# A new order for scores, raw scores, products and exponentials in three kinds of phases of a fused attention and MLP kernel

## The chip, the cores and the metric

The kernel runs on one core of one Trainium2 chip. The metric is the device time of one execution in microseconds (us), as the median of several runs. Engines are named as the profile names them: PE is TensorE (matmuls), PEld its weight loads, ACT is ScalarE, DVE is VectorE, POOL is GpSimd, SP is SyncE (here it only issues DMAs).

## The reference

One sequence of 2048 rows of width 512 goes through multi-query attention (32 heads of 16, one shared key and value head) and through an MLP with a squared ReLU; a sigmoid gate per row mixes the two.

```python
q = (x @ wq).reshape(B, S, H, Dh).transpose(0, 2, 1, 3)
k, v = x @ wk, x @ wv
scores = einsum("bhqd,bkd->bhqk", q, k) * (Dh ** -0.5)
o = einsum("bhqk,bkd->bhqd", softmax(scores, -1), v)
a = o.transpose(0, 2, 1, 3).reshape(B, S, H * Dh) @ wo
r = where(x @ w1 + b1 > 0, x @ w1 + b1, 0)
b = (r * r) @ w2 + b2
g = sigmoid((x * gate_w).sum(-1, keepdims=True))
return g * a + (1 - g) * b          # S 2048, D 512, H 32, Dh 16, F 1792
```

## The kernel before

**Units.** The attention is cut into 1024 units. A unit is one tile of 128 keys against 256 queries of four heads. Its work has three steps: two score matmuls on PE (`score`, L880; one on rows 0 to 63 of the array and one on rows 64 to 127, called row 0 and row 1 here), one exponential over all 1024 columns on ACT (L917), and four context matmuls on PE that multiply the exponentials with the values and add into `acc` (L937). The context of a unit follows its scores by four units or more (`AHEAD`).

**Two ways for a score to leave PSUM.** Most units write both score halves into one tile `s` of two banks, of which there are two (`score_part`), and the exponential reads that tile. The pool hands the two tiles out in turn, so a unit's score must wait until the exponential of the unit two before it in that turn has read its tile. The other units are called raw scores: each half goes into `x`, a single bank (`score_copy`), DVE copies it to SBUF (L901), and the exponential later works in place in SBUF (`e<-e` in the profile). A half must wait until the copy of the half before it has read `x`.

**Products.** Beside the attention PE computes the projections and the MLP. A unit of that work is a list of 12 or 15 (sometimes 9) pairs of matmuls of half height (L1244): row 0 of the array works on the first half of the sum for one output and row 1 on the second half of the sum for the output before it. So PE's work comes in pairs: one matmul on row 0 and one on row 1 at the same time.

**Phases.** The program is a row of phases (`phase`). A phase of n units and m products first issues all its pairs, then the contexts of n units. The order of the pairs and that of the exponentials on ACT come from the table `PLANS`, written out by hand. Its key is (units, products, kind). Its text has one word per step: `M` is a product on both rows, `S3` a score of unit 3 of this phase on both rows, `06` the half on row 0 of unit 6 as a raw score, and `16` the half on row 1. Words that start with 0 go to row 0 alone, those with 1 to row 1 alone, all others to both; so a word with 1 shifts row 1 by one place against row 0 until a word with 0 evens it out. The tuple behind the text is the order in which ACT takes the units' exponentials. PE, ACT and DVE each run their instructions in the order in which the program writes them.

In this kernel 33 phases are (9, 15), 7 are (8, 15), 17 are (8, 12) and 67 are (7, 12); 12 others lie at the two ends. The planner's clocks (`at_pe`, `at_act`, `at_dve`) decide beside which raw score a small DVE operation is written (`spend`), from estimated costs.

After a phase's pairs, DVE does the closing work of the finished product (for a hidden MLP unit L763, L764, L203 and L204; for an output L786 or L228) and ACT may round a weight tile (L534). When the last context of a block of 256 queries is done, ACT copies half of `acc` (L991).

Of the kernel before, what the change touches and what calls it, by code (L numbers as in the profile page):

```python
# [39 lines left out]
WHOLE, FIRST, SECOND, LATER = range(4)  # L40
TAIL = {40: 8, 32: 8, 24: 5, 19: 5, 14: 5, 9: 5, 4: 4}
PLANS = {
    (9, 15, WHOLE): ("S0 16 M M S1 M M M 06 S2 M M S4 M M 13 M S5 M M M M S7 03 M S8", (0, 1, 2, 4, 5, 3, 8, 7, 6)),
    (8, 15, WHOLE): ("14 S0 M M S1 M M 04 M S2 M M M 13 S5 M M M M M 03 M S6 S7 M", (0, 1, 2, 5, 4, 3, 6, 7)),
    (7, 15, WHOLE): ("14 S0 M M S1 M M 04 M M S2 M M 13 M M M S5 M M M S6 M M 03", (0, 1, 2, 4, 5, 3, 6)),
    (8, 12, WHOLE): ("15 S0 M M S1 M M 05 M S2 M M M S4 13 M M S6 M M 03 S7", (0, 1, 2, 4, 5, 3, 6, 7)),
    (7, 12, WHOLE): ("14 S0 M M S1 M M 04 M M S2 M M 13 M M M S5 M S6 03", (0, 1, 2, 4, 5, 3, 6)),
    (6, 12, WHOLE): ("M 02 S0 M S1 M M M M M S3 M M M S4 12 M M S5", (0, 1, 3, 4, 5, 2)),
    (6, 12, LATER): ("S0 M M S1 M M M 02 M S3 M M M S4 M 12 M M S5", (0, 1, 3, 4, 5, 2)),
# [1409 lines left out]
```

## Time and profile before

| | |
|---|---|
| median of 3 runs | 1185.44 us (1181.39 to 1188.18) |
| profiled execution | 1181.19 us, of which the span from first to last instruction 1179.4 us |
| granted PE clock in it | 0.999 |
| PE busy | 1170.9 us (99% of the span) |
| ACT busy | 1025.9 us (87%) |
| DVE busy | 687.6 us (58%) |
| POOL busy | 71.2 us (6%) |

The profile is one execution. In a timeline row stand the start in us from the span's start, the length, the engine, the line, the operation, the tiles (out<-in), the shape and how many equal ones were merged, and in brackets the idle time of the engine before it with what ended it. In the table of groups stand busy time in us and the mean of one in ns. A matmul that waits for its buffer while it is at the head of PE's queue shows as a longer matmul.

### The profile page before, as it was taken

What the parts mean: (1) busy time and instruction counts of PE and PEld (TensorE: products, weight loads), DVE (VectorE), ACT (ScalarE), POOL (GpSimd) and SP (SyncE); (2) the same over time, 40 slices, a digit from 0 to 9 for tenths busy, and PEclk for the clock granted to TensorE, in tenths of its full rate; (3) what the DMA queues carried; (4) which work ended last, traced back from release to release, by engine and by line L of the source; (5) the groups of instructions that cost most, each with busy time, mean ns of one, the idle gap of its engine ahead of it and who ended that gap; (6) DMA issues with size and microseconds to landing.
All of it is one profiled execution on the core that took longest, in us unless ns stands there. A gap on an engine that the chain in (4) does not pass through costs nothing.

```text
span 1179.4 us, 31993 instructions
## 1 busy us (share of the span) xinstructions
PE 1170.9 (99%) x13807; PEld 775.6 (66%) x13807; DVE 687.6 (58%) x1154; ACT 1025.9 (87%) x1133; POOL 71.2 (6%) x128
## 2 busy tenths in 40 slices
PE   9999999999999999999999999999999999999997
PEld 4666666666666666666666666666666666666664
DVE  6887786764754745553666636535646437444553
ACT  7798899998988888889888898988888989889884
POOL 1010110010100000100000000001000000001000
PEclk9999999999999999999999999999999999999999
DMA  7455445251433514320524305224115224322101
GB/s 253 130 157 174 136 128 201 91 196 58 166 125 110 177 39 140 99 84 7 159 95 149 101 19 176 83 65 163 61 41 180 65 65 136 104 77 75 56 37 39
DMA packets 53802, 130.28 MB, mean 110 GB/s; under 512 B 14219, under 2 KB 14715, under 8 KB 53145
## 3 DMA queue, kind: packets, MB, share of 16 engines
q1 hardware_dynamic: 38712, 90.67, 24.4%
q0 software_dynamic: 14656, 37.19, 9.4%
q8 instruction: 110, 1.80, 0.6%
q14 instruction: 36, 0.29, 0.1%
q10 hardware_dynamic: 288, 0.33, 0.1%
HBM read 87.91 MB, written 35.64 MB: 105 GB/s over the span
## 4 chain that ended last, share of the span: by engine, by line
PE 98%; ACT 1%; DVE 0%; issue 0%; DVEq 0%; ACTq 0%
PE acc L937 39%; PE mm L1244 33%; PE s L880 19%; PE x L880 5%; ACT e L917 0%; PE acc L570 0%; PE mm L211 0%; PE mm L312 0%; DVE ot L1204 0%; DVE e L901 0%; PE s L321 0%; PE acc L357 0%; PE s L211 0%; PE acc L354 0%; PE s L312 0%
## 5 line engine op out<-in xcount | busy, mean ns | idle before, releaser
L917 ACT ACTIVATE e<-s 128x1024 f32<-128x1024 f32 x765 | 744.5, 1023 | 88.9 <-PE s L880 87.6
L901 DVE COPY e<-x 128x512 f32<-128x512 f32 x518 | 358.4, 692 | 448.6 <-PE x L880 323.3
L937 PE MATMUL acc<-e,v_ext 128*32 128x256 f32 x8192 | 470.2, 381 | 0.0
L880 PE MATMUL s<-qa,k_aug 49*128 49x512 f32 x1530 | 425.2, 413 | 0.1
L937 PEld LDWEIGHTS acc<-e,v_ext 128*32 128x32 f32 x8192 | 252.3, 110 | 190.5 <-issue 38.0
L917 ACT ACTIVATE e<-e 128x1024 f32<-128x1024 f32 x259 | 273.3, 1058 | 29.0 <-DVE e L901 29.0
L880 PEld LDWEIGHTS s<-qa,k_aug 49*128 49x128 f32 x1530 | 218.2, 184 | 103.5 <-ACT e L917 70.7
L1244 PE MATMUL mm<-w2p,hr 64*128 64x512 f32 x1128 | 243.4, 392 | 0.0
L880 PE MATMUL x<-qa,k_aug 49*128 49x512 f32 x518 | 213.4, 412 | 0.1
L1244 PEld LDWEIGHTS mm<-w2p,hr 64*128 64x128 f32 x1128 | 157.4, 186 | 18.0
L1244 PE MATMUL mm<-xragain,w1p 64*128 64x512 f32 x448 | 121.1, 394 | 0.0
L880 PEld LDWEIGHTS x<-qa,k_aug 49*128 49x128 f32 x518 | 95.2, 184 | 31.5 <-DVE e L901 13.6
L1244 PE MATMUL mm<-xr,w1p 64*128 64x512 f32 x448 | 115.7, 393 | 0.0
L1244 PEld LDWEIGHTS mm<-xragain,w1p 64*128 64x128 f32 x448 | 69.9, 186 | 5.8
L1244 PEld LDWEIGHTS mm<-xr,w1p 64*128 64x128 f32 x448 | 68.1, 186 | 6.3
L1244 PE MATMUL mm<-xlagain,w1p 64*128 64x512 f32 x224 | 68.0, 393 | 0.0
L1244 PE MATMUL mm<-xl,w1p 64*128 64x512 f32 x224 | 65.3, 392 | 0.0
L1244 PE MATMUL mm<-more 64*128 64x512 f32 x216 | 59.4, 393 | 0.0
L763 DVE TENSOR_SCALAR big<-mm,b1t 128x512 f32<-128x512 f32 x56 | 41.6, 743 | 0.5 <-PE mm L1244 0.5
L764 DVE TENSOR_TENSOR big<-big 128x512 f32<-128x512 f32 x56 | 38.8, 692 | 1.9
L1244 PE MATMUL mm<-wor,orr 64*128 64x512 f32 x120 | 38.4, 393 | 0.0
L1244 PE MATMUL mm<-wor,orl 64*128 64x512 f32 x120 | 38.1, 391 | 0.0
(187 smaller groups left out, 797.8 us busy)
## 6 DMA issues: line engine op xcount, KB each, us to landing
w1p<-w1kept SPq DMA_DIRECT2D x42, 512.0 KB
w2p<-w2kept SPq DMA_DIRECT2D x35, 512.0 KB
qa<-qs SPq DMA_DIRECT2D x186, 64.0 KB
w1kept<-w1p POOLq DMA_DIRECT2D x14, 512.0 KB, 4.3
w2kept<-w2p POOLq DMA_DIRECT2D x12, 512.0 KB, 5.9
qs<-qr SPq DMA_DIRECT2D x16, 256.0 KB
ress<-res POOLq DMA_DIRECT2D x4, 1024.0 KB, 4.7
qs<-ql POOLq DMA_DIRECT2D x15, 256.0 KB, 8.1
```

The source lines that it names most:

```text
L763: nc.vector.tensor_scalar(h[0], p, b1t[:, f:f + 1], 0.0, op0=OP.add, op1=OP.max)
L764: nc.vector.tensor_tensor(h[0], h[0], h[0], OP.mult)
L880: nc.tensor.matmul(dst.rearrange("p (a n) -> p a n", a=2), k_aug[rows, kt * 128:(kt + 1) * 128], qa[it][rows, :, q * HC:q * HC + HC], star ...
L901: nc.vector.tensor_copy(e_half(u)[:, 2 * r:2 * r + 2], x.rearrange("p (a n) -> p a n", a=2))
L917: nc.scalar.activation(e_half(u), src, AF.Exp, scale=SCALE)
L937: nc.tensor.matmul(accs[q][h * 32:(h + 1) * 32], v_ext[:, kt], es[u][:, h % 2 * 2 + h // 2], start=kt == 0 and it > 0, stop=kt == NK - 1, ...
L1244: nc.tensor.matmul((self.before if r else self).bank, a[p], b[p], start=not r and i == 0, stop=r == 1 and i == len(self.terms[1]) - 1, ski ...
```

## The change

Three entries of `PLANS` get a new text and a new order of exponentials. The set of words of each text is the same.

```diff
-    (9, 15, WHOLE): ("S0 16 M M S1 M M M 06 S2 M M S4 M M 13 M S5 M M M M S7 03 M S8", (0, 1, 2, 4, 5, 3, 8, 7, 6)),
-    (8, 15, WHOLE): ("14 S0 M M S1 M M 04 M S2 M M M 13 S5 M M M M M 03 M S6 S7 M", (0, 1, 2, 5, 4, 3, 6, 7)),
+    (9, 15, WHOLE): ("S0 16 M S1 M M M M 06 S2 M M S4 M M M S5 13 M M M M S7 M 03 S8", (0, 1, 2, 4, 5, 7, 3, 8, 6)),
+    (8, 15, WHOLE): ("14 S0 M S1 M M M 04 M M S2 M M 13 M S5 M M M M M 03 M S6 S7", (0, 1, 2, 5, 4, 3, 7, 6)),
...
-    (8, 12, WHOLE): ("15 S0 M M S1 M M 05 M S2 M M M S4 13 M M S6 M M 03 S7", (0, 1, 2, 4, 5, 3, 6, 7)),
+    (8, 12, WHOLE): ("S0 15 M M S1 M M 05 S2 M M M S4 13 M M M S6 M M 03 S7", (0, 1, 2, 4, 5, 6, 3, 7)),
```

Three places show what this makes of the program. The first is PE in the phase of eight units and twelve products that stands at 620.36 us in the trace of before. These are the rows from the raw score 15 to the raw score 05 (`x<-`), before the change; `s<-` are halves of scores, `mm<-` products.

```order
L880 MATMUL x<-qa,k_aug 128x512
L1244 MATMUL mm<-xragain_4368,w1p 128x512
L880 MATMUL s<-qa,k_aug 128x512
L1244 MATMUL mm<-xlagain_4369,w1p 128x512
L1244 MATMUL mm<-w2p,hr 128x512
L880 MATMUL s<-qa,k_aug 128x512
L1244 MATMUL mm<-w2p,hr 128x512
L1244 MATMUL mm<-xragain_4368,w1p 128x512
L880 MATMUL s<-qa,k_aug 128x512
L1244 MATMUL mm<-xlagain_4369,w1p 128x512
L1244 MATMUL mm<-w2p,hr 128x512
L880 MATMUL x<-qa,k_aug 128x512
```

Here are the same rows, from 15 to 05, with the change.

```order
L880 MATMUL x<-qa,k_aug 128x512
L1244 MATMUL mm<-xlagain_4369,w1p 128x512
L1244 MATMUL mm<-w2p,hr 128x512
L880 MATMUL s<-qa,k_aug 128x512
L1244 MATMUL mm<-w2p,hr 128x512
L1244 MATMUL mm<-xragain_4368,w1p 128x512
L880 MATMUL s<-qa,k_aug 128x512
L1244 MATMUL mm<-xlagain_4369,w1p 128x512
L1244 MATMUL mm<-w2p,hr 128x512
L880 MATMUL x<-qa,k_aug 128x512
```

Ten matmuls stood between the two raw scores and eight stand there now: the second half of S0 is ahead of 15, and one product fewer is between.

The second place is PE in the phase of nine units and fifteen products at 1012.91 us, from S4 (first row) to the second half of S5 (last row), before the change.

```order
L880 MATMUL s<-qa,k_aug 128x512 x2
L1244 MATMUL mm<-w2p,hr 128x512 x5
L880 MATMUL x<-qa,k_aug 128x512
L880 MATMUL s<-qa,k_aug 128x512
L1244 MATMUL mm<-w2p,hr 128x512
L1244 MATMUL mm<-more 128x512
L880 MATMUL s<-qa,k_aug 128x512
```

With the change, from S4 to S5 and the raw score 13 behind it:

```order
L880 MATMUL s<-qa,k_aug 128x512 x2
L1244 MATMUL mm<-w2p,hr 128x512 x6
L880 MATMUL s<-qa,k_aug 128x512 x2
L1244 MATMUL mm<-more 128x512
L880 MATMUL x<-qa,k_aug 128x512
```

The raw score 13 went behind S5, and the two halves of S5 stand in one pair.

The third place is ACT in the same phase: the last six of its nine exponentials before the change. The first two rows are units 4 and 5, `e_13476` is unit 3, `e_13544` unit 8, `e_13543` unit 7 and `e_13479` unit 6.

```order
L917 ACTIVATE e_13477<-s_13506 128x1024
L917 ACTIVATE e_13478<-s_13518 128x1024
L917 ACTIVATE e_13476<-e_13476 128x1024
L917 ACTIVATE e_13544<-s_13540 128x1024
L917 ACTIVATE e_13543<-s_13530 128x1024
L917 ACTIVATE e_13479<-e_13479 128x1024
```

With the change (`e_13535` is unit 7 and `e_13545` unit 8):

```order
L917 ACTIVATE e_13477<-s_13506 128x1024
L917 ACTIVATE e_13478<-s_13516 128x1024
L917 ACTIVATE e_13535<-s_13530 128x1024
L917 ACTIVATE e_13476<-e_13476 128x1024
L917 ACTIVATE e_13545<-s_13542 128x1024
L917 ACTIVATE e_13479<-e_13479 128x1024
```

Unit 7 went ahead of the raw score's unit 3, and unit 8 behind both.

The instructions of each engine are the same in number and kind. SP's and POOL's stand in the same order as before. On ACT only exponentials change places among themselves. On DVE small operations (L960, L966, L969, L683, L686) stand one or two copies earlier or later at eleven places.

## The prediction

> **What bounds the kernel now.** I read the page first: is one engine full, and does the chain of work that ended last stay on it?
>
> ```profile
> span 1179.4 us, 31993 instructions
> ...
> PE 1170.9 (99%) x13807; PEld 775.6 (66%) x13807; DVE 687.6 (58%) x1154; ACT 1025.9 (87%) x1133; POOL 71.2 (6%) x128
> ...
> PE 98%; ACT 1%; DVE 0%; issue 0%; DVEq 0%; ACTq 0%
> ...
> L917 ACT ACTIVATE e<-s 128x1024 f32<-128x1024 f32 x765 | 744.5, 1023 | 88.9 <-PE s L880 87.6
> ```
>
> It does: TensorE (PE) carries 98% of the chain. The change leaves the number of its instructions alone, so it can only win or lose the short stretches in which TensorE stands before a matmul whose buffer is not free. Those do not show as idle time, since a waiting matmul counts as busy; they show as idle time of the weight loads (PEld) in the view of waits (total, times, longest, in us):
>
> ```profile
> PEld s L880 <- ACT e L917: 70.7, 244, 0.5
> ...
> PEld x L880 <- DVE e L901: 13.6, 79, 0.5
> ```
>
> Weight loads run ahead of the matmuls, so most of the 70.7 us costs nothing. What it costs is read from the length of a phase, as the timeline of TensorE has it (start, length, instruction). First a phase that the change does not touch, seven units beside twelve products, 19 pairs of matmuls:
>
> ```profile
> 466.79 0.50 PE L880 MATMUL s<-qa,k_aug 49*128 49x512 f32 x1
> ...
> 471.09 0.39 PE L880 MATMUL x<-qa,k_aug 49*128 49x512 f32 x1
> 471.41 3.23 PE L937 MATMUL acc<-e,v_ext 128*32 128x256 f32 x56
> ```
>
> From its first matmul to the contexts (L937) 4.62 us, 0.32 of it behind the last pair. Now one of nine units, 24 pairs:
>
> ```profile
> 1012.91 0.50 PE L880 MATMUL s<-qa,k_aug 49*128 49x512 f32 x2
> ...
> 1013.25 0.39 PE L880 MATMUL x<-qa,k_aug 49*128 49x512 f32 x1
> ...
> 1013.95 0.40 PE L880 MATMUL s<-qa,k_aug 49*128 49x512 f32 x1
> ...
> 1014.65 0.40 PE L880 MATMUL x<-qa,k_aug 49*128 49x512 f32 x1
> ...
> 1014.89 0.40 PE L880 MATMUL s<-qa,k_aug 49*128 49x512 f32 x2
> ...
> 1015.58 0.44 PE L880 MATMUL s<-qa,k_aug 49*128 49x512 f32 x2
> 1015.86 0.85 PE L1244 MATMUL mm<-w2p,hr 64*128 64x512 f32 x5
> ...
> 1016.56 0.40 PE L880 MATMUL s<-qa,k_aug 49*128 49x512 f32 x1
> ...
> 1016.81 0.40 PE L880 MATMUL s<-qa,k_aug 49*128 49x512 f32 x1
> ...
> 1018.44 0.44 PE L880 MATMUL s<-qa,k_aug 49*128 49x512 f32 x2
> 1018.81 4.09 PE L937 MATMUL acc<-e,v_ext 128*32 128x256 f32 x72
> ```
>
> Between the two copied scores (x, at 1013.25 and 1014.65) lie six pairs without a wait: 1.40 / 6 = 0.233 us a pair. Five pairs more than the seven-unit phase make 4.62 + 5 x 0.233 = 5.785; the phase took 5.90, so 0.115 is waiting. Its places: S4 at 1015.58 lasts 0.44 for 0.40, and the next pair comes after 0.28 (0.05 too late); S5 at 1016.56 (0.01); S8 at 1018.44, with 0.37 to the contexts for 0.32 (0.05).
>
> The chain in order of time has the contexts of nine-unit phases as pieces of their own (start, length):
>
> ```profile
> 946.84 4.02 PE acc L937 x72
> 957.09 4.03 PE acc L937 x72
> 967.01 4.02 PE acc L937 x72
> ```
>
> Nine contexts take 4.02, 0.447 each.
>
> ACT and DVE of the nine-unit phase, then a phase of eight units beside twelve products (20 pairs) with its ACT, then one of eight beside fifteen (23 pairs):
>
> ```profile
> 1013.45 4.88 ACT L917 ACTIVATE e<-s 128x1024 f32<-128x1024 f32 x5
> 1019.12 1.06 ACT L917 ACTIVATE e<-e 128x1024 f32<-128x1024 f32 x1 [0.79 <-DVE e L901]
> ...
> 1021.89 1.06 ACT L917 ACTIVATE e<-e 128x1024 f32<-128x1024 f32 x1
> ```
>
> ```profile
> 1013.75 0.69 DVE L901 COPY e<-x 128x512 f32<-128x512 f32 x1 [1.06 <-PE x L880]
> ```
>
> ```profile
> 620.36 0.50 PE L880 MATMUL s<-qa,k_aug 49*128 49x512 f32 x1
> ...
> 621.87 0.39 PE L880 MATMUL x<-qa,k_aug 49*128 49x512 f32 x1
> ...
> 622.32 0.45 PE L880 MATMUL s<-qa,k_aug 49*128 49x512 f32 x2
> ...
> 624.10 0.50 PE L880 MATMUL s<-qa,k_aug 49*128 49x512 f32 x1
> ...
> 624.44 0.39 PE L880 MATMUL s<-qa,k_aug 49*128 49x512 f32 x1
> ...
> 625.49 3.66 PE L937 MATMUL acc<-e,v_ext 128*32 128x256 f32 x64
> ```
>
> ```profile
> 621.19 3.77 ACT L917 ACTIVATE e<-s 128x1024 f32<-128x1024 f32 x4 [0.31 <-PE s L880]
> ```
>
> ```profile
> 261.64 0.50 PE L880 MATMUL s<-qa,k_aug 49*128 49x512 f32 x1
> ...
> 263.59 0.47 PE L880 MATMUL s<-qa,k_aug 49*128 49x512 f32 x2
> ...
> 267.25 0.42 PE L937 MATMUL acc<-e,v_ext 128*32 128x256 f32 x4
> ```
>
> Eight beside twelve: 625.49 - 620.36 = 5.13, against 4.62 + 0.233 = 4.853 without waits: 0.277, of which S2 (0.45 long) has 0.05 and S6 at 624.10 (0.50 long, its pair 0.09 late to begin with) 0.20. Eight beside fifteen: 5.61 against 5.55: 0.06, at S2 (0.47 long). The program has 33, 17 and 7 of these phases, so all the waiting that the change could take away is 33 x 0.115 + 17 x 0.277 + 7 x 0.06 = 3.8 + 4.7 + 0.4 = **8.9 us**, 0.75%.
>
> **What a wait is made of.** An exponential takes 1.02 us (page), and back to back they step by (3.77 - 1.02) / 3 = 0.92. The x tile shows the price of a buffer that comes late:
>
> ```profile
> 283.54 0.69 DVE L901 COPY e<-x 128x512 f32<-128x512 f32 x1 [0.86 <-PE s L880]
> ```
>
> ```profile
> 284.29 0.49 PE L880 MATMUL x<-qa,k_aug 49*128 49x512 f32 x1
> ```
>
> The copy ends at 284.23; the next x lasts 0.49 for 0.39, so it really ran from 284.39: a freed buffer is usable 0.16 us later. A score's exponential starts 0.50 after the score's second half (1016.81 to 1017.31, where the fifth of the group at 1013.45 begins: 1013.45 + 4.88 - 1.02). Two s tiles alternate: S2 and S5 take that of S0, S4 and S7 that of S1, S8 that of S5; in the twelve-product phase S4 follows S1, S6 follows S2. These rules give back the waits above. Nine units: exponential 1 starts at 1.04 + 0.50 = 1.54 after the phase's start, ends 2.56, plus 0.16 is 2.72, and S4 stood ready at 2.67: 0.05. Twelve products: exponentials at 0.83, 1.75 and 2.66; the third ends 3.68, plus 0.16 is 3.84, and S6 ran from 3.74 + 0.10.
>
> **The change part by part.** No instruction is added or removed on any engine. SP's and POOL's queues stand as they did; ACT's other work keeps its place; eleven small DVE operations stand one or two copies away from where they were (places below).
>
> *Nine units.* S1 goes one pair forward: its second half at 0.81, ready 1.31, so exponential 1 follows exponential 0 (0.54, from 1013.45) at ACT's pace: 1.46, ends 2.48, S4 may go at 2.64 and is due at 2.67. That wait goes (0.05). Exponential 2 hangs on S2, which stays: 1.98 + 0.50 = 2.48, ends 3.50, S5 may go at 3.66. S5 is due at 3.60 now: 0.06. Exponentials 4 and 5 run at 3.40 and 4.32 (4.40 before, since S5's second half came a pair later), the last ends 5.34, S8 may go at 5.50 and is due at 5.47 + 0.06 = 5.53: none. 0.06 stays of 0.115: 33 x 0.055 = **1.8 us**. Between ends: nothing (if exponential 0 starts 0.06 later, S4's wait stays) and 3.8. The fourth copied half (03) goes back one pair, so unit 3's exponential would start 0.23 later; that of unit 7 is put ahead of it, into the 0.79 in which ACT waited for that copy. ACT then ends the phase's exponentials some 0.7 us sooner than 1021.89 + 1.06. Nothing waits for that end, so I price it at nothing: unit 3 is the eighth context of nine, due some 5.84 + 7 x 0.447 = 9.0 us after the start, and its exponential ends near 7.5.
>
> *Eight beside twelve.* S0 stands ahead of 15, whole in the first pair, so its exponential starts at 0.54 as in the nine-unit phase, not 0.83. Exponential 1 then hangs on S1's second half, 1.04 + 0.50 = 1.54; 2 at 2.46, ends 3.48, S6 may go at 3.64 and is due at 3.60 or later. S4 may go at 2.72. All the waits for s go. But 15 is in the second pair now, as 16 is in the nine-unit phase, where the copy runs from 0.84 to 1.53 (1013.75, 0.69 long). The x tile is usable at 1.69, and 05 is still in the seventh pair, at 621.87 - 620.36 = 1.51: a **new wait of 0.18**, the same tile's, with every product behind it queued too. It delays S4 and S6 past their own waits. 0.277 - 0.18 = 0.097, times 17: **1.65 us**. Ends: nothing and 4.7.
>
> [...]
>
> *Eight beside fifteen.* S2 goes from pair 8 to pair 9 (due 2.19, its tile free near 2.0), and S5 one pair later: the 0.06 goes, 7 x 0.06 = **0.4 us**. S7's exponential ahead of S6's changes nothing by then.
>
> *DVE operations moved.* Each is at most 0.68 us and off the path unless it delays a copy; eleven places by at most 0.33 (below) would be 3.6, none would be 0. I take 0, since DVE is busy 58%.
>
> Sum: 1.8 + 1.65 + 0.4 = 3.85, say **3.8 us**. The profiled execution (span 1179.4, time 1181.19) would take 1177.4; the runs' median of 1185.44 lies 4.3 above it, and from there the forecast is **1181.6 us**, 0.32% faster. About 0.5%, 5.9 us, is what a measurement of this kernel can tell from no change.
>
> **Rivals.**
>
> *The x wait is not paid* (products behind it run first): 1.8 + 4.7 + 0.4 = 6.9, 1178.5 us. For it: 79 waits of weight loads for the x tile sum to 13.6 us, few of which cost anything. Against it: the wait at 284.29 lengthened the matmul itself by 0.10, and 624.44 came late behind S6. 0.17.
>
> *It does not do what it says*: ACT keeps its pace in nine units (exponential 0 at 0.60), and the x wait, lengthened by a DVE operation, eats all of the 0.277: 0.4, 1185.0 us. For it: S5's wait grows in my own sum. 0.15.
>
> *Slower: the first copy of nine-unit phases comes late.* With 03 a pair later DVE starts the phase's closing work 0.23 later, and the next phase's 16 can be held up. The chain above has one disturbed phase: 10.25 from contexts to contexts for 9.92, 0.33 lost; I take that as the price. If 32 of 33 phases lost that, 10.6 - 3.8 = 6.8 slower, 1192.2 us; it decides from 0.12 us a phase (3.8 / 33). Against it: DVE idles 0.86 and 1.06 before the copies shown, and some 4.3 us lie between the end of 03's copy (6.41) and the next 16's (9.87 + 0.84). 0.08.
>
> **How the numbers follow.** Forecast 0.60, rivals 0.17, 0.15, 0.08. The first two rivals lie at 1178.5 and 1185.0; the known runs spread 3 to 4 us about their median (1181.39 to 1188.18). The range 1176.6 to 1187.0 holds these, and leaves out the third and the tails. Faster by over 0.5% (below 1179.5): the first rival and a little of the forecast, 0.20. Slower by over 0.5%: 0.07. Within: 0.73.
>
> **What would show it.** In nine-unit phases: 5.84 to the contexts, S4 at its 0.40, ACT without the idle 0.79 before the copied unit. In eight beside twelve: first exponential 0.54 after the start, S6 at 0.39, 05 stretched to nearly 0.6, and 5.03 in all. In eight beside fifteen: 5.55. I am wrong if 05 is not stretched (then faster), if S4 and S6 stay stretched, or if first copies start later than 0.85.

## The result, and the profile after

| | before | changed |
|---|---|---|
| first comparison, six runs each: median | 1185.87 us (1181.14 to 1188.18) | 1177.97 us (1177.77 to 1180.41) |
| its ratio | | 0.9944, 95% interval 0.9919 to 0.9969 |
| second comparison, 35 and 13 runs: median | 1181.78 us (1181.10 to 1188.07) | 1178.29 us (1177.76 to 1189.75) |
| its ratio | | 0.9971, interval 0.9954 to 0.9988 |
| profiled execution | 1181.19 us, span 1179.4 | 1180.41 us, span 1178.6 |

The forecast was 1181.6 us, 0.32% or 3.8 us faster. The first comparison shows twice that, the second 0.29% or 3.5 us. The lowest times differ by 3.4 us in both (1181.14 and 1177.77; 1181.10 and 1177.76). The two profiled executions, though, differ by 0.8 us alone. So there are two things to explain: the 3.4 us, and what moves medians and single executions by as much again.

The page of the changed kernel, with the lines that answer to those of before:

```profile
span 1178.6 us, 32006 instructions
...
PE 1168.3 (99%) x13807; PEld 783.5 (66%) x13807; DVE 687.3 (58%) x1154; ACT 1022.4 (87%) x1133; POOL 71.3 (6%) x128
...
PE 97%; DMA 1%; ACT 1%; DVE 1%; issue 0%; ACTq 0%
```

New in the chain is the 1% of DMA, which before did not have. The view of waits, weight loads alone:

```profile
PEld s L880 <- ACT e L917: 41.2, 130, 0.8
...
PEld x L880 <- DVE e L901: 17.6, 77, 1.8
```

Waits for exponentials fell from 70.7 to 41.2 us and from 244 to 130; waits for copies of raw scores rose from 13.6 to 17.6. From the first changed phase on the second sum rose from 11.6 to 14.4; the rest of the rise, with the longest wait of 1.8, belongs to the disturbance shown below.

**The changed phases.** The timeline of TensorE in the nine-unit phase that stood at 1012.91 before:

```profile
1012.44 0.50 PE L880 MATMUL s<-qa,k_aug 49*128 49x512 f32 x2
...
1015.10 0.41 PE L880 MATMUL s<-qa,k_aug 49*128 49x512 f32 x2
...
1016.03 0.45 PE L880 MATMUL s<-qa,k_aug 49*128 49x512 f32 x2
...
1017.95 0.40 PE L880 MATMUL s<-qa,k_aug 49*128 49x512 f32 x2
1018.28 0.42 PE L937 MATMUL acc<-e,v_ext 128*32 128x256 f32 x4
```

S4 (1015.10) lasts 0.41 for 0.44 and S8 (1017.95) 0.40 for 0.44; S5 (1016.03) lasts 0.45: it has the wait that is left. 5.84 us to the contexts for 5.90. ACT in the same phase:

```profile
1012.98 4.78 ACT L917 ACTIVATE e<-s 128x1024 f32<-128x1024 f32 x5
1017.92 1.02 ACT L917 ACTIVATE e<-s 128x1024 f32<-128x1024 f32 x1 [0.16 <-PE s L880]
1018.88 1.06 ACT L917 ACTIVATE e<-e 128x1024 f32<-128x1024 f32 x1
```

Unit 7 fills the 0.79 us in which ACT waited for the copy of unit 3, and the group `e<-e` lost its waits for DVE (29.0 us before, 0.6 now, in the page's groups). A phase of eight units beside twelve products, TensorE and then DVE:

```profile
476.26 0.50 PE L880 MATMUL s<-qa,k_aug 49*128 49x512 f32 x2
...
476.61 0.39 PE L880 MATMUL x<-qa,k_aug 49*128 49x512 f32 x1
...
477.85 0.50 PE L880 MATMUL x<-qa,k_aug 49*128 49x512 f32 x1
477.85 0.50 PE L1244 MATMUL mm<-wor,orr 64*128 64x512 f32 x1
478.19 0.39 PE L880 MATMUL s<-qa,k_aug 49*128 49x512 f32 x2
...
480.02 0.39 PE L880 MATMUL s<-qa,k_aug 49*128 49x512 f32 x1
...
481.31 0.42 PE L937 MATMUL acc<-e,v_ext 128*32 128x256 f32 x4
```

```profile
477.11 0.69 DVE L901 COPY e<-x 128x512 f32<-128x512 f32 x1 [2.59 <-PE x L880]
```

S2 (478.19) and S6 (480.02) have their plain 0.39 now. The stretched one is the raw score 05 at 477.85, 0.50 long: the copy before it ends at 477.80, and 477.80 + 0.16 = 477.96 is where it really ran, 0.19 behind its place (476.26 + 1.51 = 477.77). 5.05 to the contexts for 5.13. In the phases of eight units beside fifteen products 5.56 for 5.61.

**The disturbance.** The chain between 85 and 130 us, long before the first changed phase, has a piece that before has not:

```profile
94.33 12.32 DMA stage<-in_xs
```

```profile
106.67 0.69 DVE L669 SCALAR_TENSOR_TENSOR stage<-stage,gwb 128x512 f32<-128x512 f32 x1 [2.10 <-DMA stage<-in_xs]
```

The rows of x for the gate's sums landed 12.32 us after their issue. The issue itself stands at 94.33 where before has 91.96, so that DVE was ready for them 106.67 - 2.10 - 94.33 = 10.2 us behind it. DVE stood 2.10 us at the head of its queue waiting for them, the raw scores' copies stood behind, and TensorE behind these: 1.34 us idle ahead of the raw score at 108.03, the first matmul of the phase at 105.02. Before, the two stand at 105.48 and 103.97, so the rows cost 3.01 - 1.51 = 1.5 us. Another 1.05 were lost ahead of that (105.02 for 103.97), where ACT waited for an earlier transfer out of its buffer:

```profile
89.79 0.38 ACT L991 ACTIVATE accs<-acc 128x256 f32<-128x256 f32 x1 [1.46 <-DMA lq<-accs]
```

The whole of it is read from the first contexts of the first changed phase. In the chain they are one piece; here it is before, then after:

```profile
248.90 3.59 PE acc L937 x64
```

```profile
251.53 3.59 PE acc L937 x64
```

Up to there after is 2.6 us late, with the same program. From there to the end of the span it takes 1178.6 - 251.5 = 927.1 us, before 1179.4 - 248.9 = 930.5: **3.4 us** less, as the lowest times say.

### The profile page after: what moved, and what is told of

The parts are those of the page before. It is cut to its first block, busy times and chain, and to the rows that moved or that the text cites. A ratio compares the mean times of both kernels' runs of the same rounds, so it can differ in the third digit from the quotient of the medians.

```text
span 1178.6 us, 32006 instructions
## 1 busy us (share of the span) xinstructions
PE 1168.3 (99%) x13807; PEld 783.5 (66%) x13807; DVE 687.3 (58%) x1154; ACT 1022.4 (87%) x1133; POOL 71.3 (6%) x128
## 4 chain that ended last, share of the span: by engine, by line
PE 97%; DMA 1%; ACT 1%; DVE 1%; issue 0%; ACTq 0%
PE acc L937 39%; PE mm L1244 33%; PE s L880 18%; PE x L880 5%; DMA stage<-in_xs 1%; ACT e L917 1%; PE acc L570 0%; PE mm L211 0%; PE mm L312 0%; DVE ot L1204 0%; DVE e L901 0%; PE s L321 0%; PE acc L357 0%; PE s L211 0%; PE acc L354 0%
## 5 line engine op out<-in xcount | busy, mean ns | idle before, releaser
L880 PE MATMUL s<-qa,k_aug 49*128 49x512 f32 x1530 | 407.8, 410 | 0.6 <-ACT e L917 0.4
L880 PEld LDWEIGHTS s<-qa,k_aug 49*128 49x128 f32 x1530 | 213.4, 184 | 86.3 <-ACT e L917 41.2
L1244 PEld LDWEIGHTS mm<-w2p,hr 64*128 64x128 f32 x1128 | 160.3, 186 | 18.9
L880 PEld LDWEIGHTS x<-qa,k_aug 49*128 49x128 f32 x518 | 95.2, 184 | 36.9 <-DVE e L901 17.6
L991 ACT ACTIVATE accs<-acc 128x256 f32<-128x256 f32 x60 | 23.1, 385 | 28.6 <-PE acc L937 25.5
```

What stands on the lines that cost most here:

```text
L880: nc.tensor.matmul(dst.rearrange("p (a n) -> p a n", a=2), k_aug[rows, kt * 128:(kt + 1) * 128], qa[it][rows, :, q * HC:q * HC + HC], star ...
L991: nc.scalar.activation(a[:, q * HC:q * HC + HC], acc, AF.Copy)
L1244: nc.tensor.matmul((self.before if r else self).bank, a[p], b[p], start=not r and i == 0, stop=r == 1 and i == len(self.terms[1]) - 1, ski ...
```

## The experiments

### Both kernels again, and more time for the gate's rows

e1 is the kernel of before and e2 the changed one, with no edit. e3 and e4 are the same two with one edit, which plans the sums further behind their loads:

```diff
-                landed[i] = max(at_dve, at_pe) + 3 * LANDS
+                landed[i] = max(at_dve, at_pe) + 5 * LANDS
```

> The kernel of before, unchanged. The trace of after lost about 2.8 us in the stretch from 88 to 120 us, where DVE waited for the rows of the gate (L661), and that stretch is the same program in both kernels. Theory A: the change itself is worth 3.4 to 3.8 us, and the rest of the 7.9 us between the medians is such waiting for DMAs, which some executions of either kernel have and others don't. Then the times here split into some near 1181.2 and some at 1185 to 1188, and in a profiled execution of the long sort the lost time stands before 243 us, where the first changed phase begins, with DVE behind a DMA. Rival B: the change takes away waits in the changed phases that only some executions of before have. Then a long execution has nine-unit phases longer than 5.90 us or eight-unit ones longer than 5.13 us.

> The changed kernel, once more. Theory A: most times near 1177.8, as many executions of 1180 to 1185 among them as chance gives; lowest time 3.4 to 3.8 us under the lowest of before. Rival B: no time over 1180.5, and the median 7 to 8 us under that of before.

> The kernel of before, with the sums of the gate's rows planned 30 us behind their loads in place of 18 (L661 to L669). Theory A: if DVE's wait for these rows makes the long executions, nearly all times here lie within 1 us of 1181.2, and the median is 4 to 5 us under that of before. Rival C: the long executions come from another DMA (the weights of the MLP, L490, or the reloads of q), and the times here split as those of before do.

> The changed kernel with the same 30 us. Theory A: all times within 1 us of 1177.8, 3.4 to 3.8 us under the same kernel with the old order. Rival B: 7 to 8 us under it.

| | runs | lowest | median | over 3 us above its lowest | ratio to before |
|---|---|---|---|---|---|
| before, beside them | 35 | 1181.10 | 1181.78 | 8 | |
| e1 | 12 | 1181.21 | 1181.60 | 3 | 0.9999 (0.9982 to 1.0016) |
| e2 | 13 | 1177.76 | 1178.29 | 5 | 0.9971 (0.9954 to 0.9988) |
| e3 | 12 | 1180.60 | 1181.02 | 1 | 0.9987 (0.9971 to 1.0003) |
| e4 | 12 | 1178.62 | 1178.90 | 0 | 0.9966 (0.9952 to 0.9981) |

e2's profiled execution is its longest, 1189.75 us. Chain, DVE, and the piece that marks the first changed phase:

```profile
100.07 14.28 DMA stage<-in_xs
```

```profile
114.37 0.69 DVE L669 SCALAR_TENSOR_TENSOR stage<-stage,gwb 128x512 f32<-128x512 f32 x1 [2.61 <-DMA stage<-in_xs]
```

```profile
260.85 3.59 PE acc L937 x64
```

It reached the first changed phase 12 us late, and from there took 1188.0 - 260.85 = 927.1 us, to the tenth the same as the other execution. Of the 12 us, 6.7 were lost before the rows were even asked for. The first block of contexts (48 records, eight to a unit) stands in the chain of before, and in that of e2, at

```profile
33.30 2.73 PE acc L937 x48
```

```profile
39.97 2.73 PE acc L937 x48
```

and the windows of e2 (length, then busy time and count of PE, PEld, DVE, ACT and POOL, granted clock, DMA share, GB/s) say why:

```profile
25.00:30.00 5.00, 5.00 (x18) 3.82 (x16) 2.39 (x6) 2.79 (x4) 0.00 (x0) 0.50 0.77 265
30.00:35.00 5.00, 5.00 (x29) 4.08 (x29) 2.23 (x6) 3.03 (x5) 0.00 (x0) 0.50 0.61 199
```

The granted clock was 0.50 for these ten microseconds, where before shows 1.00. The windows on both sides show 0.90 (20 to 25 us) and 0.73 (35 to 40). Counted as a mix of 1.00 and 0.50 they make 1.0 + 10 + 2.7 = 13.7 us at 0.50, an estimate, and half of that, 6.8, is about what was lost. The other 5.3 us were lost between 92 and 120 us. ACT and TensorE first:

```profile
97.42 0.38 ACT L991 ACTIVATE accs<-acc 128x256 f32<-128x256 f32 x1 [2.38 <-DMA oc<-accs]
```

```profile
98.77 0.50 PE L880 MATMUL s<-qa,k_aug 49*128 49x512 f32 x2 [1.30 <-ACT e L917]
```

That took 1.5 us (TensorE's phases begin 6.7 late ahead of it and 8.25 behind it). The wait for the rows took 2.0: the first matmul of that phase stands at 112.22 and its second raw score at 115.73, where before has 103.97 and 105.48. And 1.7 went by the clock behind that wait, as the last section shows.

e1's profiled execution took 930.5 from that piece on (1179.7 - 249.17), as before's did. So rival B is out: what makes a changed kernel's execution long stands ahead of the change, and it hits that kernel as well as before (5 of 13 in e2, 0 of 6 at first, 11 of 47 for before in this comparison). The four of six in the first measurement of before were bad luck, and made the first ratio too good. No long execution of before itself was profiled, so for before the place is inferred from the program ahead of 243 us being the same.

More time for the rows helps as theory A says, but not wholly: 1 long execution in 24 here, and none in the 12 of e10 below (e9 beside it has one), while 55 of 210 runs of the kernels with 18 us were long (all comparisons after the first). e3's median is 0.8 us under that of before and not the 4 to 5 that were expected, because the median of before had itself fallen to 1181.78. Rival C has a part too: 1.5 of e2's 12 us are its, and in a long execution of e5 below it is nearly all, with no wait for the rows behind it:

```profile
91.65 0.38 ACT L991 ACTIVATE accs<-acc 128x256 f32<-128x256 f32 x1 [3.32 <-DMA oc<-accs]
```

So what is late is not one transfer but several of those under way between 85 and 115 us. e4 was to lie within 1 us of 1177.8 and does not: its median is 1178.90, its lowest 0.9 above the changed kernel's; three of its phases are longer by 0.3 each, all with a copy of a raw score later than DVE's other work lets it be.

Such late copies stand in the other kernels too, at places that change from one text to another. Before has two, in the phases at 726.24 and 950.79; the second is the disturbed phase of the prediction. In the second the raw score's matmul starts at 951.13 and DVE is idle, yet the copy comes 0.89 us later, where 0.50 is usual:

```profile
952.02 0.69 DVE L901 COPY e<-x 128x512 f32<-128x512 f32 x1 [3.72 <-PE x L880]
```

The two phases take 4.96 for 4.62 and 6.23 for 5.90. e3 has the phases of before unchanged, and yet neither of the two copies is late: from the first contexts of the first phase of eight beside fifteen, the first that the change touches, it takes 1178.8 - 249.1 = 929.7 us, 0.8 under before, 0.7 of it in these two phases. The changed kernel has neither of them, but one at another place (970.24, 4.96 us). So some 0.4 of its 3.4 us are a side effect that an edit without the new order brings as well. What makes these copies late was not found.

### One entry at a time

e5 has the new entry for (9, 15) alone, e6 that for (8, 12) alone.

```diff
-    (9, 15, WHOLE): ("S0 16 M M S1 M M M 06 S2 M M S4 M M 13 M S5 M M M M S7 03 M S8", (0, 1, 2, 4, 5, 3, 8, 7, 6)),
+    (9, 15, WHOLE): ("S0 16 M S1 M M M M 06 S2 M M S4 M M M S5 13 M M M M S7 M 03 S8", (0, 1, 2, 4, 5, 7, 3, 8, 6)),
```

```diff
-    (8, 12, WHOLE): ("15 S0 M M S1 M M 05 M S2 M M M S4 13 M M S6 M M 03 S7", (0, 1, 2, 4, 5, 3, 6, 7)),
+    (8, 12, WHOLE): ("S0 15 M M S1 M M 05 S2 M M M S4 13 M M M S6 M M 03 S7", (0, 1, 2, 4, 5, 6, 3, 7)),
```

> The entry for nine units beside fifteen products alone has its new form. Theory: 33 nine-unit phases shrink from 5.90 to 5.84 us to the contexts and nothing else moves, so 1.8 us under before (near 1179.5 where no DMA disturbs). Rival: the new order of exponentials, which ends ACT's work of a phase 0.7 us sooner, also helps the phase behind it; then 3 us or more.

> The entry for eight units beside twelve products alone has its new form. Theory: 17 phases shrink from 5.13 to 5.06 us, 1.2 us under before, with the x wait of 0.18 to 0.2 at the raw score 05 in place of the waits at S2 and S6. Rival: these phases keep 5.13 when the nine-unit phases ahead of them keep their old form.

e5: 0.9975 (0.9955 to 0.9994), lowest 1179.58, nine-unit phases 5.85 (median of 33), the others as before by their medians. From the first changed phase to the end 1181.6 - 252.9 = 928.7 us, 1.8 under before. e6: 0.9983 (0.9966 to 1.0001), lowest 1179.38, phases of eight beside twelve 5.06 (median of 17), the nine-unit ones 5.90. To the end 1178.2 - 249.2 = 929.0, 1.5 under before. Each entry brings its own part, both rivals fall, and 1.8 + 1.5 with the 0.4 of the third entry (7 x 0.06, not run alone) is 3.7, near the 3.4. The late copies are in these sums: e6 lost the one of the disturbed phase, 0.3 of its 1.5, and its 17 phases won the 1.2 that were expected; e5 lost both and has three other phases that are 0.2 to 0.3 longer.

### The raw score 05 earlier and later

Both start from the changed kernel: e7 puts 05 and S2 one pair later, e8 puts 05 one pair earlier.

```diff
-"S0 15 M M S1 M M 05 S2 M M M S4 13 M M M S6 M M 03 S7"
+"S0 15 M M S1 M M M 05 S2 M M S4 13 M M M S6 M M 03 S7"
```

```diff
-"S0 15 M M S1 M M 05 S2 M M M S4 13 M M M S6 M M 03 S7"
+"S0 15 M M S1 M 05 M S2 M M M S4 13 M M M S6 M M 03 S7"
```

> The changed kernel, with the raw score 05 and S2 one pair later in the 17 phases of eight units beside twelve products. Theory: 05 is due at 1.74 us then and the x tile is free at 1.70, so its wait goes; S4 waits 0.05 for exponential 1; the phase takes 4.91 us to the contexts, and the whole 17 x 0.15 = 2.5 us less than the changed kernel, near 1175.3 undisturbed. Rival (the x wait costs nothing by itself, the 0.2 are those of the s tiles): no change, 5.06.

> The changed kernel, with 05 one pair earlier in the same phases. Theory: due at 1.27 us and served at 1.70, it waits 0.42; S4 and S6 find their tiles free; 5.27 us to the contexts, 17 x 0.21 = 3.6 us more than the changed kernel. Rival (products run past a waiting raw score): 5.06, no change.

TensorE and the copy ahead of 05 in e8, then TensorE in e7, each in the phase shown above:

```profile
475.93 0.50 PE L880 MATMUL s<-qa,k_aug 49*128 49x512 f32 x2
...
477.51 0.50 PE L880 MATMUL x<-qa,k_aug 49*128 49x512 f32 x1 [0.17 <-DVE e L901]
...
481.22 0.42 PE L937 MATMUL acc<-e,v_ext 128*32 128x256 f32 x4
```

```profile
476.76 0.69 DVE L901 COPY e<-x 128x512 f32<-128x512 f32 x1 [2.60 <-PE x L880]
```

```profile
474.14 0.50 PE L880 MATMUL s<-qa,k_aug 49*128 49x512 f32 x2
...
475.85 0.40 PE L880 MATMUL x<-qa,k_aug 49*128 49x512 f32 x1
...
476.77 0.47 PE L880 MATMUL s<-qa,k_aug 49*128 49x512 f32 x2
477.08 0.45 PE L880 MATMUL x<-qa,k_aug 49*128 49x512 f32 x1
...
479.07 0.42 PE L937 MATMUL acc<-e,v_ext 128*32 128x256 f32 x4
```

In e8 the copy ends at 477.45 and 05 runs from 477.61 (0.16 later), 0.41 behind its place at 1.27: 5.29 to the contexts in this phase and as median, for 5.27 expected. Lowest 1181.51, 3.7 over the changed kernel, for 3.6. The whole gain of the change is gone by one pair. Products did not run past the waiting raw score here: the one paired with it starts at 477.51 too, and the next pair at 477.85.

In e7 05 lasts its plain 0.40: its wait is gone. But the phase takes 4.93 (median 4.96), not 4.91, and the lowest time is 1176.40, 1.4 under the changed kernel where 2.5 were expected. The next waits stand in the rows: S4 at 476.77 lasts 0.47, as foreseen, and the raw score 13 right behind it 0.45, which was not: 13 is five pairs behind 05 now. e7 is the fastest kernel of this study: 0.9957 (0.9936 to 0.9978), median 1176.98. The lowest times of e7 and e8 come from another comparison than the changed kernel's, in which before's own lowest was 0.3 lower (1180.82 for 1181.10). Counted against that, e8 costs 4.0 and e7 wins 1.1.

### S4 and the raw score 13 later as well

e9 tries to take S4's wait from e7, e10 is e9 with the longer time for the gate's rows.

```diff
-"S0 15 M M S1 M M M 05 S2 M M S4 13 M M M S6 M M 03 S7"
+"S0 15 M M S1 M M M 05 S2 M M M S4 13 M M S6 M M 03 S7"
```

> The kernel with 05 and S2 one pair later, and S4 and 13 one pair later as well, in the 17 phases of eight units beside twelve products. There S4 waited 0.06 for exponential 1 (it was due at 2.66 and its tile free at 2.71). Theory: due at 2.90 it doesn't wait; S7, whose tile is freed by exponential 4 at 4.55, is due at 4.53: 4.88 us to the contexts, 17 x 0.08 = 1.4 us less than with S4 at its old place and 3.0 less than the changed kernel. Rival: the wait only moves on to S6 or S7, 4.96.

> The same, with the sums of the gate's rows planned 30 us behind their loads in place of 18. Theory: fewer long executions than the same kernel with 18 (at most 1 in 12 over 3 us above the lowest), the lowest time within 1 us of it. Rival: the long executions come from other DMAs, and are as many.

```profile
476.65 0.41 PE L880 MATMUL s<-qa,k_aug 49*128 49x512 f32 x2
...
477.36 0.44 PE L880 MATMUL s<-qa,k_aug 49*128 49x512 f32 x1
...
478.17 0.49 PE L880 MATMUL x<-qa,k_aug 49*128 49x512 f32 x1
```

```profile
477.42 0.69 DVE L901 COPY e<-x 128x512 f32<-128x512 f32 x1 [0.81 <-PE x L880]
```

These are TensorE and DVE of e9 in the same phase. S4 (476.65) no longer waits, but S6 (477.36) does, and 03 (478.17, 0.49 long) waits for the copy of 13, which ends at 478.11: 13 came one pair later and 03 did not. The phases take 5.08 (median), no better than the changed kernel, and the time is 1178.44 (0.9965, 0.9949 to 0.9981). My 4.88 was wrong, because I had looked at the s tiles alone; the rival named S6 but not the x tile. e10: 12 runs from 1178.57 to 1179.93, none long, and its lowest within 0.7 of e9's: as theory A has it.

### Text and order of exponentials apart

e11 takes the new order of exponentials for (9, 15) and keeps the old text, e12 the reverse; both start from before.

```diff
-    (9, 15, WHOLE): ("S0 16 M M S1 M M M 06 S2 M M S4 M M 13 M S5 M M M M S7 03 M S8", (0, 1, 2, 4, 5, 3, 8, 7, 6)),
+    (9, 15, WHOLE): ("S0 16 M M S1 M M M 06 S2 M M S4 M M 13 M S5 M M M M S7 03 M S8", (0, 1, 2, 4, 5, 7, 3, 8, 6)),
```

```diff
-    (9, 15, WHOLE): ("S0 16 M M S1 M M M 06 S2 M M S4 M M 13 M S5 M M M M S7 03 M S8", (0, 1, 2, 4, 5, 3, 8, 7, 6)),
+    (9, 15, WHOLE): ("S0 16 M S1 M M M M 06 S2 M M S4 M M M S5 13 M M M M S7 M 03 S8", (0, 1, 2, 4, 5, 3, 8, 7, 6)),
```

> The kernel of before; of the nine-unit entry only the order of exponentials is new (7 ahead of 3 and 8), the text is the old one. Theory: nothing waits for the end of ACT's exponentials in these phases, so they keep 5.90 us to the contexts and the time stays within 0.5 us of before. Rival: the order carries the gain, 5.84 to 5.86, 1.5 us less.

> The kernel of before; of the nine-unit entry only the text is new, the order of exponentials is the old one (3 ahead of 8 and 7). Theory: unit 3's exponential waits for the later 03 until 6.45 us and ACT ends its nine at 10.27, 0.40 into the next phase, whose first exponential is due at 0.54; so most phases have the 5.84 of the changed entry, and only those in which ACT also copies acc (0.39 us) start their exponentials late, by 0.2 to 0.3 us, and grow past 5.90. Rival: the order is free to choose, all phases 5.84.

e11: 0.9997 (0.9977 to 1.0018), nine-unit phases 5.90 (median of 33). e12: 0.9973 (0.9958 to 0.9988), 5.85. In the nine-unit phases the text carries the gain, the order does not. The whole of e11 is not within the 0.5 us that I had allowed: its lowest time, 1180.31, is 0.6 under before's 1180.88, and from the first contexts of its phase of eight beside fifteen to the end it takes 1178.6 - 249.1 = 929.5 us, 1.0 under before. Of that 0.7 are the two late copies of before, which it lost as e3 did with the old order. ACT of e12:

```profile
1010.97 1.06 ACT L917 ACTIVATE e<-e 128x1024 f32<-128x1024 f32 x1
1011.91 0.39 ACT L991 ACTIVATE accs<-acc 128x256 f32<-128x256 f32 x1
1012.17 4.71 ACT L917 ACTIVATE e<-s 128x1024 f32<-128x1024 f32 x5
1018.00 1.06 ACT L917 ACTIVATE e<-e 128x1024 f32<-128x1024 f32 x1 [1.12 <-DVE e L901]
```

ACT idles 1.12 us before unit 3 again, and its work runs into the next phase, up to 1012.03 where that phase begins at 1011.56. But even with the copy of `acc` behind it the first exponential starts at 1012.17, 0.61 after the phase's start, and this phase takes 5.86. My expectation that the phases with that copy would grow past 5.90 failed: the operations overlap on ACT here (the copy starts at 1011.91, ahead of 1012.03), and the 0.39 of the copy delays what follows by 0.26 (1011.91 to 1012.17).

## Why the prediction was right

**The mechanism and the sum.** Every term was read as waits of TensorE in one kind of phase. The gain is there, in those phases (medians, to the contexts):

| phases | before | forecast | measured | forecast gain | measured gain |
|---|---|---|---|---|---|
| 33 of nine beside fifteen | 5.90 | 5.84 | 5.84 | 1.8 | 33 x 0.054 = 1.8 |
| 17 of eight beside twelve | 5.13 | 5.03 | 5.06 | 1.65 | 17 x 0.074 = 1.26 |
| 7 of eight beside fifteen | 5.61 | 5.55 | 5.56 | 0.4 | 7 x 0.058 = 0.4 |

The sum measured so is 3.45, for 3.85. Added up phase by phase over the two traces, the three kinds win 2.1, 1.1 and 0.3; 0.4 of the 2.1 is the disturbed phase, whose late copy e3 lost without the change. So the waits that the change took away are worth 3.1, and that the lowest times show 3.4 is in part luck.

**The base.** The forecast time of 1181.6 started from a median of three runs of which two were long. From the profiled execution the same sum gave 1177.4, and the median of the changed kernel, 1177.97, lies near that, 3.6 under the forecast. That it lies next to the first rival's 1178.5, and that it is over 0.5% faster, comes from this base and not from the rival.

**What was sized wrong.** The new wait of 05 is some 0.20 and not 0.18 (0.277 - 0.074; 0.19 in the phase shown): most copies of the raw score ahead of it end 1.53 to 1.56 after the phase's start, and the copy that I took ended at 1.53. 05 shows as 0.50 long, not nearly 0.6, since its start is late too (last section). The first exponential starts at 0.61 there (476.87 in the phase shown), not 0.54; as the x wait comes first, S4 and S6 still find their tiles free. In nine-unit phases S4 keeps a wait of some 0.02 where I had none, and S5 has less than my 0.06.

**The terms set to nothing.** That nothing in the nine-unit phases waits for the end of ACT's exponentials is shown by e11 and e12. No run moved the eleven DVE operations alone, but no cost of them is seen: the 46 seven-unit phases from the first changed phase on sum as before, one 0.34 shorter and one 0.33 longer by a late copy that went or came. The disturbed nine-unit phase, which I took as a price, lost its 0.33 in the changed kernel.

**The rivals.** That products queue behind a waiting raw score was assumed in the forecast; what spoke for it in the trace of before is that the pair behind S6's first half came 0.34 after it (624.10 to 624.44) and not 0.233. That the x wait is not paid falls with e8, which paid 0.41 in full. That the change does not do what it says falls with e5 and e6. First copies do not come late in the changed kernel's nine-unit phases: they start 0.77 to 0.88 us into the phase, and the longest of the 33 takes 5.87 to the contexts. The first measurement lay outside "within 0.5%" for another reason than any of these: executions that were long ahead of the change were many among the first six of before.

## What to carry to other kernels

When one engine is full, as TensorE is here (99% of the span), a new order of its work is worth what its waits are worth (here 3.1 of the 3.4 us), and these are read as stretched instructions and as the length of a stage against one of the same kind without waits. Add the round trip of each buffer before moving two of its users closer: here 0.50 + 0.69 + 0.16 = 1.35 us for the raw-score tile, six pairs of matmuls, and every place with five pairs (05 in the change, 13 in e7, 03 in e9) showed a wait. The text of before has five between 13 and 03 as well; there S6 waits in between and makes the room (03 at 624.91 lasts 0.41). Before a difference of medians is believed, compare lowest times and the stretch of the trace that the change can reach; in e2 a wait of 2.0 us outside that stretch cost 3.7, with the granted clock at 0.55 and 0.60 in the 4 us behind it.

## What the runs showed of the hardware

A load of 512 KB of rows took 12.32 and 14.28 us to land in two executions whose DVE waited for it (in e8's profiled execution it waited 1.8 us for the same rows); TensorE stood 1.34 us behind the first and 1.85 behind the second. 18 us were planned between load and use, but DVE was ready 10.2 and 11.7 us behind the issue. In the second, e2, the wait was not all. TensorE's first matmul after it, and the windows behind it:

```profile
115.73 0.49 PE L880 MATMUL x<-qa,k_aug 49*128 49x512 f32 x1 [1.85 <-DVE e L901]
```

```profile
116.00:118.00 2.00, 2.00 (x12) 1.58 (x12) 0.95 (x3) 0.46 (x1) 0.00 (x0) 0.55 0.46 164
118.00:120.00 2.00, 2.00 (x14) 1.55 (x12) 1.15 (x2) 1.51 (x2) 0.00 (x0) 0.60 0.46 161
120.00:122.00 2.00, 2.00 (x34) 1.08 (x34) 1.50 (x5) 1.69 (x2) 0.00 (x0) 1.00 0.22 83
```

After an idle 1.85 us the granted clock was 0.55 and 0.60 in the next two windows: pairs of matmuls came 0.43 us apart (116.38, 116.81, 117.23), where before has 0.23 (105.71, 105.95, 106.17). Counted as a mix of 1.00 and of the 0.50 of the other rows, the two windows make 1.8 + 1.6 = 3.4 us at 0.50, an estimate; half of that is the 1.7 us that were lost behind the wait. The same is seen in e5, where TensorE idles 2.23 us up to 93.00, behind ACT's wait for `oc<-accs`:

```profile
94.00:96.00 2.00, 2.00 (x12) 1.58 (x10) 0.69 (x1) 1.72 (x2) 0.48 (x1) 0.50 0.70 179
```

The windows on both sides of it show 0.91 and 0.73, so counted in the same way 0.4 + 2.0 + 1.1, some 3.4 us. The wait and half of that, 2.23 + 1.7, make the 4.0 us that e5's profiled execution is late (its first contexts of the phase of eight beside fifteen start at 252.9, before's at 248.9). Behind the idle 1.34 us of the changed kernel's first execution and the 1.30 at 98.77 in e2 the clock stayed at 1.00. So e2's wait that took 2.0 us cost 3.7. What sets the length of these stretches at the low rate was not shown. What lowered the clock of e2 between 25 and 35 us was not found: TensorE's longest idle time just ahead of it in the timeline is 0.18 us, though matmuls there come up to 1.1 us later than before's (23.66 for 22.55), so that stretched ones may hide more.

The raw scores that waited for a copy in the phases shown (477.85 in the changed kernel, 477.51 in e8, 478.17 in e9) start in the trace 0.05 or 0.06 us after the copy's end, last 0.49 or 0.50 for 0.39, and the pair behind them comes 0.33 or 0.34 behind that start and not 0.233 (478.19, 477.85, 478.50). So I take the held ones to have run 0.16 behind the copy's end; their start alone does not show the wait. What made the one long execution in 36 that remains with 30 us was not settled, and a text with six pairs between all raw scores of the twelve-product phase was not tried.
